# Sliding-window attention and a gated FFN on one core: half 1's steps in another order, and batch 1's last steps earlier in tile 1

## Chip, core and metric

One core of a Trainium2 chip. The metric is the device time of one execution in microseconds; the kernel before took 249.9 (median of 4 runs, 249.57 to 251.01).

## What is computed

Attention over 4 batches, 8 heads, 768 positions, 64 elements per head, where a query sees the first 8 keys and the 96 keys up to its own, with a bias by distance; then a gated feed-forward block over all 3072 tokens.

```python
scores = scale * np.matmul(q, k.transpose(0, 1, 3, 2))
bias = -slopes[:, None, None] * dist[None, :, :]
scores = np.where(keep, scores + bias[None], -1e9)      # keep = first 8 keys, or 0 <= rel < 96
a = np.exp(scores - np.max(scores, axis=-1, keepdims=True))
a = a / (np.sum(a, axis=-1, keepdims=True) + 1e-09)
attn = np.matmul(a, v)
x = attn.transpose(0, 2, 1, 3).reshape(B * S, H * D)    # 3072 x 512
g = x @ w_gate                                          # 512 x 1536
val = x @ w_val
out = (g * (1.0 / (1.0 + np.exp(-g))) * val) @ w_out    # 1536 x 512
```

## The kernel before

**Tiles.** The feed-forward block runs over 8 tiles t of 384 tokens (half a batch each: tile 2b + half) and 12 slices f of 128 hidden elements. For each (t, f) TensorE (PE) makes a gate group (`gps`, L502) and a value group (`vps`, L502), four matmuls each; ACT makes tanh of the gate (`th`, L513), DVE `sl` from it (L515) and `hT` from the value (L519). An output part is three matmuls into `ops` (L531); four parts make 128 rows, which ACT scales (`osb`, L537) and SP stores (L538). The texts write g6, v6 and o6 for the gate group, the value group and the output part of f = 6.

**Attention** works on pairs of heads (4 to a batch) and quads (2 to a batch, two pairs each). Its steps are put between the groups of the feed-forward block:

- Batch 0 comes in two halves. `trh` turns q and k of a pair in half 1 on PE (L293); DVE copies the k part (L306) and ACT the q part (L320) out of PSUM. `sch` makes the scores of a pair in half 1: bias matmuls (L329), scores (L340), four exps on ACT (L348).
- From batch 1 on `tr` (batch 1, L267) or transposing DMAs (L397) turn, `sc` makes one of three banks of scores of a pair (L365), with exps (L373) and a mask product (L381, L384).
- `va` is a quad's values for one half: denominators and two numerators on PE (L429), copies `ns` on ACT (L460), `dT` and `dR` on DVE (L439, L440), `rb` on DVE (L445), and the two products that write two of the four pieces of `xT` (L464): on DVE for batch 0, on POOL from batch 1 on. A tile's first gate group reads all four pieces of its `xT` in turn.

**What sets the order.** The program is scheduled by hand: each engine runs its instructions in the order in which the code emits them. `stretches` (L699) is a list of (groups, steps, tail, owed). In a stretch every group adds its weight (1.0, an output part 1.1) times `quota` to `owed`, and a step is emitted whenever `owed` reaches 1:

```python
        quota = len(steps) / (work - tail)
```

So a longer tail makes the steps come at shorter intervals. Parts of a step that are off PE go to the list `later`; `run_later(1)` emits one of them before each group, and all of them before a step. For `va` these are `invert` (dT, dR), then `spread` (rb, and on POOL the two products).

**Loads.** POOL issues the loads that cast to 16 bits: in the order of the code for what comes ahead of the loop (weights, batch 0, q, k and v of batch 1; L118, L152, L170, L212, L217), and by due step for batches 2 and 3. Those of batch 2 (L721 to L731) start at t = 1, f = 7: `stage_rows` (the memset of `kend` on POOL, L160; small copies of `kend` and `kst` on SP, L161 and L164) and two loads of `kst` (L193), then at each f two loads of `qst` or `kst`, and at f = 8 also one of `kend` (L198). They are emitted at the head of the gate group of that f, ahead of its `run_later`.

**PSUM.** The steps take their buffers from four banks a0 to a3 in turn (`bank`, L233), gate and value groups from three others, output parts from one.

Of the kernel before, what the change touches and what calls it, by code (L numbers as in the profile page):

```python
# [37 lines left out]
def kernel(  # L38
# [199 lines left out]
    def banks(name, dt=FP32):  # L238
        return [bank(name, dt) for _ in range(2)]
# [401 lines left out]
    def sc(b, hp, bk):  # L641
        on_vector = b < 2 or bk < 2 or hp % 2 == 0
        return lambda: pairs[b, hp].scores(bk, nc.vector if on_vector else nc.gpsimd, bool(later))

    def va(b, g, half):
        return lambda: quads[b, g].values(half, bank, nc.vector if b == 0 else nc.gpsimd)

    def tr(b, hp):
        return pairs[b, hp].transposes

    def trh(hp):
        def step():
            pairs[0, hp].transposes_half(1, [t[:, 0:TB] for t in banks("trs", FP16)], V, A)
        return step

    def sch(hp):
        def step():
            p = pairs[0, hp]
            scs = [p.bias(1, 0), p.bias(1, 1)]
            for which in range(2):  # L660
                p.scores_half(1, which, scs[which])
        return step
# [13 lines left out]
    def first(b):  # L676
        return [[tr(b, 0), tr(b, 1)], [sc(b, 0, 0), sc(b, 0, 1)], [tr(b, 2), tr(b, 3)],
                [sc(b, 1, 0), sc(b, 1, 1)], [sc(b, 2, 0), sc(b, 2, 1)], [va(b, 0, 0)],
                [sc(b, 3, 0), sc(b, 3, 1)], [], [va(b, 1, 0)]]

    def both(b):

        n = b + 1

        return [[sc(b, 0, 2), sc(b, 1, 2)], [sc(b, 2, 2), sc(b, 3, 2), fetch(n, 0, 1)],
                [va(b, 0, 1)], [va(b, 1, 1)],
                [sc(n, 0, 0), sc(n, 0, 1), fetch(n, 2, 3)], [sc(n, 1, 0), sc(n, 1, 1)],
                [va(n, 0, 0)], [sc(n, 2, 0), sc(n, 2, 1)],
                [sc(n, 3, 0), sc(n, 3, 1)], [va(n, 1, 0)]]

    half1 = [[trh(0), trh(1)], [trh(2), trh(3)], [sch(0)], [sch(1)],
             [va(0, 0, 1)], [sch(2)], [sch(3)], [va(0, 1, 1)]]

    def ff(t, f0, f1, n_out=(0,)):
        return [(t, f, n_out[(f - f0) % len(n_out)]) for f in range(f0, f1)]
# [1 line left out]
    stretches = [  # L699
        (ff(0, 0, 4), [], 0, 0),  # L700
        (ff(0, 4, 11) + [(0, 11, 3)], half1, 4.7, 0.4),
        (ff(1, 0, 12, (0, 1, 1, 1)), first(1), 5.0, 0.2),
        (ff(2, 0, 12, (1,)) + ff(3, 0, 12, (1,)), both(1), 6.0, 0.4),
        (ff(4, 0, 12, (1,)) + ff(5, 0, 12, (1,)), both(2), 6.0, 0.4),
        (ff(6, 0, 12, (1,)), second(3), 6.0, 0.4),
# [95 lines left out]
```

The softmax here doesn't subtract the row's maximum and nothing guards it: scores larger than these inputs give would overflow.

## Time and profile before

| | |
|---|---|
| time, median of 4 runs | 249.9 us |
| the profiled execution | 249.78 us |
| its span | 248.0 us |
| PE busy | 238.5 us (96%) |
| DVE, ACT, POOL busy | 159.8, 130.1, 116.3 us |
| PE clock granted | full in all slices |
| PE idle waits on transfers and xT up to 78 us, by the list of waits | q 1.4, xT 1.1, qst 0.6, vS 0.5, wg 0.2 us |

All positions are microseconds from the span's start. A timeline line gives start, duration, engine, line, operation, output and input, the count of instructions merged, and in brackets the idle time ahead of it and what ended it. A line of waits gives the total, the number of waits and the longest. A line of POOL with DMA_DIRECT2D is the issue of a transfer, not the transfer.

### The profile page before, as it was taken

What the parts mean: (1) busy time and instruction counts of PE and PEld (TensorE: products, weight loads), DVE (VectorE), ACT (ScalarE), POOL (GpSimd) and SP (SyncE); (2) the same over time, 40 slices, a digit from 0 to 9 for tenths busy, and PEclk for the clock granted to TensorE, in tenths of its full rate; (3) what the DMA queues carried; (4) which work ended last, traced back from release to release, by engine and by line L of the source; (5) the groups of instructions that cost most, each with busy time, mean ns of one, the idle gap of its engine ahead of it and who ended that gap; (6) DMA issues with size and microseconds to landing.
All of it is one profiled execution on the core that took longest, in us unless ns stands there. A gap on an engine that the chain in (4) does not pass through costs nothing.

```text
span 248.0 us, 6076 instructions
## 1 busy us (share of the span) xinstructions
PE 238.5 (96%) x2428; PEld 135.0 (54%) x2428; DVE 159.8 (64%) x346; ACT 130.1 (52%) x289; POOL 116.3 (47%) x139
## 2 busy tenths in 40 slices
PE   7997999899998999999999999999999999999994
PEld 4454555465554555555555555555555556555543
DVE  5668656678884767766775566676766666555510
ACT  5735668776753653555734734656635534332321
POOL 8898895445099924506429678603030342200000
PEclk9999999999999999999999999999999999999999
DMA  7999999999469999921919999931001101100122
GB/s 145 167 177 165 186 154 191 202 168 130 92 48 139 128 170 121 143 63 48 90 45 95 89 153 180 175 59 44 19 26 45 42 3 42 42 17 28 42 87 86
DMA packets 86644, 25.10 MB, mean 101 GB/s; under 512 B 72800, under 2 KB 83672, under 8 KB 86616
## 3 DMA queue, kind: packets, MB, share of 16 engines
q0 software_dynamic: 67472, 14.05, 69.8%
q1 hardware_dynamic: 18584, 10.30, 18.4%
q8 instruction: 19, 0.31, 0.5%
q10 hardware_dynamic: 560, 0.36, 0.5%
q14 instruction: 9, 0.07, 0.1%
HBM read 28.67 MB, written 6.29 MB: 141 GB/s over the span
## 4 chain that ended last, share of the span: by engine, by line
PE 74%; POOL 12%; DMA 11%; issue 1%; DVE 0%; ACT 0%; POOLq 0%
PE ops L531 23%; PE vps L502 21%; PE gps L502 21%; DMA qst<-in_q_dram 5%; PE sc L365 3%; DMA q<-in_q_dram 3%; DMA vS<-in_v_dram 3%; PE num L429 3%; POOL wv L212 2%; PE den L429 2%; POOL vS L170 2%; POOL wg L212 1%; POOL xT L464 1%; POOL k L118 1%; POOL qst L193 1%
## 5 line engine op out<-in xcount | busy, mean ns | idle before, releaser
L515 DVE SCALAR_TENSOR_TENSOR sl<-th,gps 128x384 f32<-128x384 f32 x94 | 52.0, 553 | 52.3 <-ACT th L513 51.5
L513 ACT ACTIVATE th<-gps 128x384 f32<-128x384 f32 x94 | 46.3, 493 | 65.9 <-PE gps L502 64.2
L502 PE MATMUL gps<-xT,wg 128*128 128x384 f16 x376 | 77.2, 326 | 1.3 <-POOL xT L464 1.1
L502 PE MATMUL vps<-xT,wv 128*128 128x384 f16 x376 | 76.6, 326 | 0.6 <-DVE sl L515 0.6
L531 PE MATMUL ops<-wo,hT 128*128 128x512 f16 x276 | 73.1, 379 | 0.0
L519 DVE TENSOR_TENSOR hT<-vps,sl 128x384 f16<-128x384 f32 x94 | 51.9, 552 | 10.1 <-PE vps L502 2.8
L464 POOL TENSOR_TENSOR xT<-ns,rb 128x384 f16<-128x384 f32 x24 | 23.9, 1015 | 69.3 <-DVE rb L445 69.3
L502 PEld LDWEIGHTS <-wg 128*128 128x128 f16 x384 | 36.3, 98 | 33.3 <-issue 1.7
L502 PEld LDWEIGHTS <-wv 128*128 128x128 f16 x384 | 36.1, 98 | 26.9 <-issue 3.2
L531 PEld LDWEIGHTS <-hT 128*128 128x128 f16 x276 | 26.2, 98 | 23.7 <-issue 0.6
L373 ACT ACTIVATE at<-sc 128x432 f16<-128x432 f32 x72 | 33.2, 535 | 9.6 <-PE sc L365 9.6
L170 POOL DMA_DIRECT2D vS<-in_v_dram x28 | 24.8, 898 | 6.5 <-DMA kst<-in_k_dram 2.4
L537 ACT ACTIVATE osb<-ops 128x512 f32<-128x512 f32 x23 | 13.7, 597 | 17.1 <-PE ops L531 17.1
L460 ACT COPY ns<-num 128x384 f32<-128x384 f32 x28 | 12.0, 482 | 9.2 <-PE num L429 8.3
L384 DVE TENSOR_TENSOR at<-at,masks 128x864 f16<-128x864 f16 x20 | 12.1, 607 | 7.0 <-ACT at L373 7.0
L193 POOL DMA_DIRECT2D kst<-in_k_dram x16 | 14.1, 888 | 0.0
L193 POOL DMA_DIRECT2D qst<-in_q_dram x16 | 13.7, 867 | 0.0
L384 POOL TENSOR_TENSOR at<-at,masks 128x864 f16<-128x864 f16 x4 | 7.3, 1820 | 13.3 <-ACT at L373 13.3
L348 ACT ACTIVATE at<-sc 128x432 f16<-128x432 f32 (+2 forms) x32 | 11.6, 446 | 3.1 <-PE sc L340 2.9
L429 PE MATMUL num<-at,vS 128*32 128x216 f16 (+6 forms) x560 | 12.3, 226 | 0.5 <-DMA vS<-in_v_dram 0.5
L439 DVE STREAM_TRANSPOSE dT<-den 128x384 f32<-128x384 f32 x16 | 9.2, 578 | 1.6 <-PE den L429 1.5
L429 PEld LDWEIGHTS <-vS 128*32 128x32 f16 x560 | 9.7, 95 | 1.0 <-DMA vS<-in_v_dram 0.7
(71 smaller groups left out, 174.8 us busy)
## 6 DMA issues: line engine op xcount, KB each, us to landing
out_dram<-osb SPq DMA_DIRECT2D x23, 256.0 KB
vS<-in_v_dram POOLq DMA_DIRECT2D x24, 120.0 KB, 6.3
wg<-in_moe_w_gate_dram POOLq DMA_DIRECT2D x12, 128.0 KB, 5.2
wv<-in_moe_w_val_dram POOLq DMA_DIRECT2D x12, 128.0 KB, 5.0
wo<-in_moe_w_out_dram POOLq DMA_DIRECT2D x4, 384.0 KB, 9.7
qst<-in_q_dram POOLq DMA_DIRECT2D x16, 96.0 KB, 4.0
kst<-in_k_dram POOLq DMA_DIRECT2D x16, 90.0 KB, 3.8
kst<-in_k_dram POOLq DMA_DIRECT2D x2, 384.0 KB, 13.4
```

What stands on the lines that cost most here:

```text
L170: nc.gpsimd.dma_start(out=vSs[b][NG:NG + n, c, :, :], in_=v[b, :, KC * c:KC * c + n, :].rearrange("h p d -> p h d"))
L193: nc.gpsimd.dma_start(out=st[b][p0:p0 + n, h // 2, :, h % 2, :], in_=src[b, h, 0:n * J].rearrange("(t p) d -> p t d", p=n))
L373: nc.scalar.activation(out=at[:, hi, :], in_=sc[hi][:, 0:BANK], func=AF.Exp, scale=scale)
L384: mul_eng.tensor_mul(at, at, m[:, :, o:o + BANK])
L429: nc.tensor.matmul(dst[r, o:o + n], lhsT=ones[:, 0:32] if side is None else vals[:, 4 * g + j, side::2], rhs=pairs[b, 2 * g + j // 2].at[c ...
L464: mul_eng.tensor_mul(self.x_out(half, side), srcs[side], self.rb)
L502: nc.tensor.matmul(gv[f, which][:, 0:TB], lhsT=w[:, c, 128 * f:128 * f + 128], rhs=x_of(t)[:, c, :], start=(c == 0), stop=(c == NC - 1))
L513: nc.scalar.activation(out=th, in_=dst[:, 0:TB], func=AF.Tanh, scale=0.5)
L515: nc.vector.scalar_tensor_tensor(out=sl, in0=th, scalar=1.0, in1=dst[:, 0:TB], op0=AluOp.add, op1=AluOp.mult)
L519: nc.vector.tensor_mul(hTs[t][:, f, :], dst[:, 0:TB], gv["sl"])
L531: nc.tensor.matmul(ops, lhsT=hTs[t][:, f, 128 * i:128 * i + 128], rhs=wo[:, f, :], start=(f == 0), stop=(f == NFF - 1))
L537: nc.scalar.mul(out=osb, in_=ops, mul=0.5)
```

## The change

Two edits in the lists that set the order.

```diff
-    half1 = [[trh(0), trh(1)], [trh(2), trh(3)], [sch(0)], [sch(1)],
-             [va(0, 0, 1)], [sch(2)], [sch(3)], [va(0, 1, 1)]]
+    half1 = [[trh(0), trh(1)], [sch(0)], [trh(2), trh(3)], [sch(1)],
+             [sch(2)], [va(0, 0, 1)], [sch(3)], [va(0, 1, 1)]]
...
     stretches = [
         (ff(0, 0, 4), [], 0, 0),
         (ff(0, 4, 11) + [(0, 11, 3)], half1, 4.7, 0.4),
-        (ff(1, 0, 12, (0, 1, 1, 1)), first(1), 5.0, 0.2),
+        (ff(1, 0, 12, (0, 1, 1, 1)), first(1), 7.0, 0.2),
```

In half 1 the slots stay where they are and the steps in them change places. In tile 1's stretch the tail goes from 5.0 to 7.0, which moves the later steps. Worked out with `quota`, the order on PE is (steps in brackets; sc2 stands for the scores of pair 2, in tile 1 its banks 0 and 1; tr for transposes, va0 for the values of quad 0):

```
half 1 before: g4 v4 [tr0 tr1] g5 [tr2 tr3] v5 g6 [sc0] v6 g7 [sc1] v7 g8 [va0] v8 g9 [sc2] v9 g10 [sc3] v10 [va1] g11 v11 o o o
half 1 after:  g4 v4 [tr0 tr1] g5 [sc0] v5 g6 [tr2 tr3] v6 g7 [sc1] v7 g8 [sc2] v8 g9 [va0] v9 g10 [sc3] v10 [va1] g11 v11 o o o
tile 1 before: ... g5 v5 o5 [sc2] g6 v6 o6 [va0] g7 v7 o7 [sc3] g8 v8 g9 [empty] v9 o9 g10 [va1] v10 o10 g11 v11 o11
tile 1 after:  ... g5 v5 [sc2] o5 g6 [va0] v6 o6 g7 [sc3] v7 o7 g8 [empty] v8 g9 v9 [va1] o9 g10 v10 o10 g11 v11 o11
```

## Prediction

> **What bounds the kernel now.** The page first: PE is busy 96% of the span, so what an edit of order can win or lose is PE's idle time. The list of PE's own waits says where that idle time is:
>
> ```profile
> PE trs L293 <- DMA q<-in_q_dram: 1.4, 3, 0.6
> ...
> PE gps L502 <- POOL xT L464: 1.1, 2, 0.6
> PE vps L502 <- DVE sl L515: 0.6, 1, 0.6
> PE trs L267 <- DMA qst<-in_q_dram: 0.6, 1, 0.6
> PE num L429 <- DMA vS<-in_v_dram: 0.5, 1, 0.5
> ...
> PE gps L502 <- DMA wg<-in_moe_w_gate_dram: 0.2, 1, 0.2
> ...
> PE den L429 <- ACT at L348: 0.2, 1, 0.2
> ```
>
> The PE timeline dates them. In half 1: 24.34 (0.65, q), 26.47 (0.39, q), 28.45 (0.20, wg), 34.86 (0.47, vS), 41.84 (0.17, exp). At the head of tile 1: 49.35 (0.63, qst). At the head of tile 2: 76.99 and 77.94 (0.44 and 0.62, xT). From 78 to 236 us the table by stage has PE busy 22.00 of 22.00 and 136.00 of 136.00. So whatever PE gains or loses up to 78 us reaches the end one to one.
>
> The two stretches end in different waits. At 49.35 the transposes of batch 1 wait for a transfer:
>
> ```profile
> 49.35 0.53 PE L267 MATMUL trs<-ident,qst 128*64 128x128 f16 x12 [0.63 <-DMA qst<-in_q_dram]
> ```
>
> At 77.94 the first gate group of tile 2 waits for the last piece of xT, which POOL makes. POOL's timeline there shows why it is late:
>
> ```profile
> 56.98 0.55 POOL L160 MEMSET kend<- 128x512 f16 x1
> 57.50 1.67 POOL L193 DMA_DIRECT2D kst<-in_k_dram  x2
> 67.87 2.32 POOL L464 TENSOR_TENSOR xT<-ns,rb 128x384 f16<-128x384 f32 x2 [8.71 <-DVE rb L445]
> 70.14 0.69 POOL L198 DMA_DIRECT2D kend<-in_k_dram  x1
> 70.82 1.68 POOL L193 DMA_DIRECT2D qst<-in_q_dram  x2
> 72.48 1.75 POOL L193 DMA_DIRECT2D kst<-in_k_dram  x2
> 74.20 1.72 POOL L193 DMA_DIRECT2D qst<-in_q_dram  x2
> 75.90 1.99 POOL L464 TENSOR_TENSOR xT<-ns,rb 128x384 f16<-128x384 f32 x2
> ```
>
> The reader is to see two things. POOL stands 8.71 us idle before the products of the first quad, since they wait for rb. From then on it has no gap: the second pair of products starts when the loads of batch 2 ahead of it have been issued (75.90), not when its rb is ready, which was at 74.73 (74.16 + 0.57 in DVE's timeline).
>
> [...] kst and qst take POOL 0.84 to 0.92 us each and land a median of 3.5 us after issue, and POOL goes on meanwhile. [...] the first pair of products took 2.32, with a mask product of DVE (L384, at 68.72) beside it; the second pair, with none, 1.99.
>
> **Part 1, half 1's order.** No instruction is added or dropped; the engines' instruction lists of the two kernels have the same lengths. The step slots stay where they are, so scores of pair 0 now run in the slot at 25.72 (g6 and v5 stand for the gate group of f = 6 and the value group of f = 5, o5 for the output part behind it), and transposes 2 and 3 in the one at 28.78. The score step is 1.10 (28.78 to 29.88), two transposes without their wait 0.99 (25.72 to 27.10, less 0.39). The scores need pair 0's and 1's copies out of PSUM: DVE's end at 25.60 and ACT's at 25.60, so no stall. Then v5 0.66 and half of g6 0.33 bring PE to 25.72 + 1.10 + 0.66 + 0.33 = 27.81; the wg half lands at 28.45, as before, since POOL issues it without waiting for PE: a wait of 0.64 in place of 0.39 + 0.20. g6 ends at 28.78 in both. From there to the end of the last values (42.73) the work was 13.95; it loses a score step (-1.10), gains two transposes (+0.99), and the vS wait goes (-0.47), as those values now come after scores of pair 2, later than 34.86. The exp wait of 0.17 I leave. Sum: 0.58 sooner, from both sides 0 to 0.8 (where PE is early it may wait for the weights of f = 10, but those had landed by its old time).
>
> On the path this is worth **nothing**. Tile 1's first step keeps its place (after three groups), and qst lands at 49.31: it is issued at 36.69 behind a fixed POOL queue and takes 12.62. PE comes at 47.62 in place of 48.20 and waits 1.21 in place of 0.63. The same 1.21 is the cover if some copy stalls half 1: up to that much is free, beyond it each us is lost.
>
> **Part 2, tail 5.0 to 7.0 in tile 1's stretch.** The groups weigh 33.9, so a step comes every (33.9 - 7)/9 = 2.99 in place of 3.21 units. Worked through, the first four steps keep their slots; scores of pair 2 move from after o5 to after v5; values of quad 0 from after o6 to after g6; scores of pair 3 from after o7 to after g7; values of quad 1 from after g10 to after v9. PE's total does not change. What moves on POOL decides: values of quad 0 pass the loads of f = 7, so the order is now products of quad 0, **then** memset and two kst loads, then the old sequence. The products of quad 1 stay behind the f = 10 loads.
>
> So the 0.55 + 1.67 = 2.19 us (56.98 to 59.17) that lay in POOL's idle time now lie behind its wait for rb: **+2.19**. Against it, rb is ready sooner. The steps, with spacings of the trace: v5 starts at 60.45; scores start 0.74 later (57.92 to 58.66): 61.19. Exps start 0.40 after (61.84 to 62.24): 61.59. In the new order all four exps stand ahead of g6's tanh, 1.64 for four (59.16 to 60.80): 63.23. sl 0.57 after (63.18 to 63.75): 63.80. The mask product 0.47 after (61.37 to 61.84, the same pair of instructions): 64.27. dT 0.59 after (64.87 to 65.46): 64.86. dT to the end of rb, in the same order as at 72.99 to 74.73, 1.74: 66.60. It was 67.72, so **-1.12**. Both ends for this: with DVE free, den ready at about 63.5 plus 1.74 gives 65.2 (-2.5); with nothing won, 0.
>
> POOL then: 66.60 + 0.15 = 66.75 start; 2.32 for the pair[...]; 2.19; 5.71 for kend and six loads (70.19 to 75.90); 1.99. End: 78.96. It was 77.89. Queued behind: PE's fourth matmul of tile 2, with all of PE after it; SP's copies of kend and kst, behind the memset, from 65.54 to about 70, ahead of the next output at 76.89, so free. PE stall in tile 2: 1.06 grows to 2.13. Nothing later absorbs it.
>
> Sum: 0 + 2.19 - 1.12 = +1.07. Against the profiled execution's 249.78 (248.0 span and 1.78 around it): **250.85**, say 250.9. The median of the four runs, 249.9, lies 0.12 above that execution, well inside their spread.
>
> **Rivals.** (A) The stall goes as the place of the step suggests: quad 1's values run 1.3 us sooner and POOL is in time; 1.06 gone, 248.7. For it: the values do move. Against it: POOL was late because of loads, not of rb, and even with DVE free the chain gives -2.5 + 2.19 = -0.3, 249.5. (B) rb is no sooner, since DVE is at 10.34 of 12.00 between 56 and 68 and the mask product goes ahead of dT: then the full 2.19 stays and the time is 252.0. It decides when rb ends at 67.7 or later. (C) The end on the faster side, through half 1: PE is 0.58 ahead and qst lands that much sooner: 250.85 - 0.58 = 250.3. Against: nothing in POOL's queue up to 56 us waits for PE.
>
> **Chances.** Forecast 0.62, own range 250.4 to 251.4; A and its weaker form 0.10; B 0.22; C 0.06. A measurement of this kernel tells about 0.5% from no change, that is 248.65 and 251.15. Of the forecast's 0.62, 0.18 lies above 251.15: slower 0.22 + 0.18 = 0.40. Of A 0.03 lies below 248.65: faster 0.03. Same 0.57. The range, 249.8 to 252.0, leaves out most of A and the tail of B.
>
> **What would show it.** Right: qst transposes still at 49.35 with a wait of about 1.2; no vS wait; POOL's order xT, memset, kst; first xT at about 66.8; xT of quad 1 ending near 79.0; two waits on xT of about 2.1 together; PE without gap afterwards. Wrong: a first xT before 65.7 (then no loss), qst transposes before or after 49.35, or a new wait after 80 us.

## The result, and the profile after

| | before | changed |
|---|---|---|
| time, median | 249.52 us (64 runs) | 250.54 us (43 runs) |
| ratio of the times | | 1.0034, 95% interval 1.0018 to 1.0050 |
| the profiled execution | 249.78 us, span 248.0 | 250.87 us, span 249.1 |
| mean granted PE clock in it | 1.000 | 0.992 |

Ratios and means of times are of executions within 1.5% of the fastest of the same kernel, unless the text says otherwise; medians and counts of low clocks take all. The change costs about 0.9 us. The sum of the prediction (+1.07, to 250.9) is near it, but not all of its terms are, as the trace shows first. PE's own waits in the changed kernel:

```profile
PE gps L502 <- POOL xT L464: 1.8, 2, 1.2
...
PE trs L293 <- DMA q<-in_q_dram: 0.9, 2, 0.7
PE vps L502 <- DVE sl L515: 0.8, 2, 0.7
PE gps L502 <- DMA wg<-in_moe_w_gate_dram: 0.7, 1, 0.7
...
PE den L429 <- ACT at L348: 0.2, 1, 0.2
```

The waits on vS and on qst are gone, the wait on wg has come as half 1's step said, and the wait on xT has grown. Why it has grown is on POOL's timeline:

```profile
54.07 1.54 POOL L170 DMA_DIRECT2D vS<-in_v_dram  x2 [1.54 <-DMA qst<-in_q_dram]
65.10 2.32 POOL L464 TENSOR_TENSOR xT<-ns,rb 128x384 f16<-128x384 f32 x2 [9.49 <-ACT th L513]
67.36 0.52 POOL L160 MEMSET kend<- 128x512 f16 x1
67.82 1.74 POOL L193 DMA_DIRECT2D kst<-in_k_dram  x2
69.55 0.65 POOL L198 DMA_DIRECT2D kend<-in_k_dram  x1
70.19 1.69 POOL L193 DMA_DIRECT2D qst<-in_q_dram  x2
71.84 1.77 POOL L193 DMA_DIRECT2D kst<-in_k_dram  x2
73.56 1.73 POOL L193 DMA_DIRECT2D qst<-in_q_dram  x2
75.25 2.01 POOL L464 TENSOR_TENSOR xT<-ns,rb 128x384 f16<-128x384 f32 x2
```

DVE's timeline has the rb of quad 0:

```profile
64.38 0.57 DVE L445 STREAM_TRANSPOSE rb<-dR 128x384 f32<-128x384 f32 x1
```

Memset and first kst loads now stand behind the products of quad 0 (67.36 to 69.55, 2.19 us), where before they lay in POOL's idle time. POOL waits 9.49 us with nothing to do, then runs without a gap to 77.26. (The releaser named, ACT's tanh, had long been done; the wait is for rb, which ends at 64.38 + 0.57 = 64.95.)

PE's timeline at the head of tile 2, in the kernel before and then in the changed one, shows the longer stall, and something that the prediction does not have:

```profile
76.07 0.49 PE L502 MATMUL gps<-xT,wg 128*128 128x384 f16 x2
76.99 0.32 PE L502 MATMUL gps<-xT,wg 128*128 128x384 f16 x1 [0.44 <-POOL xT L464]
77.94 0.32 PE L502 MATMUL gps<-xT,wg 128*128 128x384 f16 x1 [0.62 <-POOL xT L464]
78.10 0.81 PE L502 MATMUL vps<-xT,wv 128*128 128x384 f16 x4
```

```profile
74.69 0.49 PE L502 MATMUL gps<-xT,wg 128*128 128x384 f16 x2
76.36 0.32 PE L502 MATMUL gps<-xT,wg 128*128 128x384 f16 x1 [1.19 <-POOL xT L464]
77.31 0.32 PE L502 MATMUL gps<-xT,wg 128*128 128x384 f16 x1 [0.63 <-POOL xT L464]
77.47 1.29 PE L502 MATMUL vps<-xT,wv 128*128 128x384 f16 x4
78.56 1.48 PE L531 MATMUL ops<-wo,hT 128*128 128x512 f16 x3
79.84 1.43 PE L502 MATMUL gps<-xT,wg 128*128 128x384 f16 x4
81.10 0.81 PE L502 MATMUL vps<-xT,wv 128*128 128x384 f16 x4
```

The groups right behind the stall take 1.29 to 1.48 us in place of 0.81. (The bracket counts only the gap after the modelled end of the matmul before. The gate group as a whole took 78.10 - 76.07 = 2.03 us before and 77.47 - 74.69 = 2.78 in the changed kernel, against 0.65 without a wait, so a stall listed as 1.06 costs 1.38, and one of 1.82 costs 2.13.) The table by stage, with the granted clock in the column behind POOL's, says why:

```profile
core 0: us, PE busy (x) PEld busy (x) DVE busy (x) ACT busy (x) POOL busy (x), PEclk, DMA share, GB/s
77.00:77.50 0.50, 0.19 (x2) 0.12 (x2) 0.00 (x0) 0.00 (x0) 0.50 (x2) 1.00 1.51 325
77.50:81.00 3.50, 3.50 (x12) 1.50 (x11) 1.11 (x2) 0.49 (x1) 3.50 (x5) 0.52 1.22 128
81.00:81.50 0.50, 0.50 (x5) 0.27 (x3) 0.00 (x0) 0.20 (x1) 0.50 (x2) 0.92 2.22 141
```

From 77.67 to 81.08 us, 3.41 us, PE ran at half its clock (0.50 in each of the slices 78 to 79, 79 to 80 and 80 to 81). From the last xT wait to the end of the span the kernel before takes 248.0 - 77.94 = 170.06 us, the changed one 249.1 - 77.31 = 171.79: the fall costs 1.73 us. Without it this execution would have been faster than the profiled one before, and that leads to the other surprise, at the head of tile 1:

```profile
47.03 0.53 PE L267 MATMUL trs<-ident,kst 128*64 128x128 f16 x12
47.49 0.53 PE L267 MATMUL trs<-ident,qst 128*64 128x128 f16 x12
```

The transposes of q start at 47.49 without a wait. The prediction had put them at 49.35, on a landing (the moment when a transfer's data have arrived) taken for fixed.

### The profile page after: what moved, and what is told of

It is laid out like the page before. It is cut to its first block, busy times and chain, and to the rows that moved or that the text cites. A ratio compares the mean times of both kernels' runs of the same rounds, so it can differ in the third digit from the quotient of the medians.

```text
span 249.1 us, 6075 instructions
## 1 busy us (share of the span) xinstructions
PE 239.8 (96%) x2428; PEld 135.4 (54%) x2428; DVE 160.2 (64%) x346; ACT 129.8 (52%) x289; POOL 116.3 (47%) x139
## 4 chain that ended last, share of the span: by engine, by line
PE 77%; POOL 4%; issue 1%; ACT 0%
PE ops L531 24%; PE gps L502 22%; PE vps L502 22%; PE sc L365 3%; PE num L429 3%; PE den L429 2%; PE trs L267 1%; POOL qst L193 1%; POOL kst L193 1%; POOL xT L464 1%; PE ops L547 1%; POOL kend L198 0%; POOL kend L160 0%; ACT th L513 0%; ACT osb L551 0%
## 5 line engine op out<-in xcount | busy, mean ns | idle before, releaser
L502 PEld LDWEIGHTS <-wg 128*128 128x128 f16 x384 | 36.8, 98 | 35.4 <-issue 3.0
L429 PE MATMUL num<-at,vS 128*32 128x216 f16 (+6 forms) x560 | 11.9, 226 | 0.0
```

The source lines that it names most:

```text
L429: nc.tensor.matmul(dst[r, o:o + n], lhsT=ones[:, 0:32] if side is None else vals[:, 4 * g + j, side::2], rhs=pairs[b, 2 * g + j // 2].at[c ...
L502: nc.tensor.matmul(gv[f, which][:, 0:TB], lhsT=w[:, c, 128 * f:128 * f + 128], rhs=x_of(t)[:, c, :], start=(c == 0), stop=(c == NC - 1))
```

## The experiments

Three theories came out of the trace. **Loads**: the loads that POOL issues ahead of a product decide when tile 2 can start. **Clock**: a stall of PE at that place lets the clock fall in some executions. **Lead**: batch 1's q lands at varying times, so part of half 1's lead reaches the end, against the prediction's "worth nothing". In the table "low clock" counts executions with a mean granted clock of 0.993 or less: 3.41 us at half the clock take 0.7% off the mean of a span of 248 us, and the changed kernel's trace, with these 3.41 us, has 0.992. (A mean of 0.998 or 0.999 is not counted: f1's trace has 0.998, and 1.00 in the stage behind its stall, 77 to 81 us.)

| run | half 1 | tail | loads | xT stall in its trace | ratio to before, 95% interval | low clock |
|---|---|---|---|---|---|---|
| e1_same_again | old | 5 | as before | 1.1 | 1.0018 (0.9998 to 1.0037) | 5 of 22 |
| e2_half1_only | new | 5 | as before | 1.1 | 1.0001 (0.9981 to 1.0021) | 1 of 22 |
| e3_tail_only | old | 7 | as before | 1.8 | 1.0092 (1.0057 to 1.0126) | 4 of 9 |
| e4_loads_ahead | new | 7 | f = 7 at f = 6 | 0 | 0.993 (0.990 to 0.996) | 0 of 12 |
| f1_changed_again | new | 7 | as before | 1.8 | 1.0028 (1.0002 to 1.0053) | 9 of 22 |
| f2_kept_busy | new | 7 | as before | filled | 1.0015 (0.9992 to 1.0038) | 0 of 22 |
| f3_tail_loads_ahead | old | 7 | f = 7 at f = 6 | 0 | 0.9949 (0.9926 to 0.9972) | 1 of 21 |
| f4_before_loads_behind | old | 5 | f = 10 at f = 11 | 0.2 | 0.9939 (0.9917 to 0.9962) | 0 of 22 |
| g1_half1_again | new | 5 | as before | 1.1 | 0.9957 (0.9932 to 0.9982) | 0 of 22 |
| g2_ahead_again | new | 7 | f = 7 at f = 6 | 0 | 0.9898 (0.984 to 0.9955) | 0 of 6 |
| g3_ahead_old_half1 | old | 7 | f = 7 at f = 6 | 0 | 0.9952 (0.9924 to 0.998) | 0 of 17 |
| g4_behind_half1 | new | 5 | f = 10 at f = 11 | 0.2 | 0.9941 (0.9914 to 0.9968) | 0 of 19 |

The e, the f and the g runs were each made on one chip, the three on different ones.

### The two parts apart

The kernel before, unchanged (no edit):

> The kernel before, unchanged, beside itself: ratio 1.000, so its interval tells what five rounds can resolve. Its trace is a second sample of what varies from run to run. Theory 1 (the transfer of batch 1's q lands at a fixed place, 49.3 us, with PE waiting 0.6 us for it): the same wait again. Theory 2 (its landing varies by a microsecond or two between executions): another wait, or none, and everything after it shifted by that much. The clock should be full throughout, with a stall of about 1.1 us on xT at the head of tile 2.

1.0018, with an interval to 1.0037, so differences under 0.2 to 0.4% are not to be read from one such run. Its trace has the stall of 1.1 us at tile 2 and a wait for batch 1's q of 0.34 us (at 49.76), in place of 0.63.

Half 1's order alone:

```diff
-    half1 = [[trh(0), trh(1)], [trh(2), trh(3)], [sch(0)], [sch(1)],
-             [va(0, 0, 1)], [sch(2)], [sch(3)], [va(0, 1, 1)]]
+    half1 = [[trh(0), trh(1)], [sch(0)], [trh(2), trh(3)], [sch(1)],
+             [sch(2)], [va(0, 0, 1)], [sch(3)], [va(0, 1, 1)]]
```

> Half 1's new order alone, tail 5.0 as before. Theory 1 (the prediction: PE's lead of 0.6 us is lost in the wait for batch 1's q): ratio 1.000, 249.5 us. Theory 2 (that landing varies and is often earlier, so the lead counts): 0.3 to 0.6 us faster, ratio 0.998. In the trace both have g6's wait on weights at about 0.7 us, no vS wait, and the last values of half 1 about 0.6 us sooner; the stall at tile 2 stays at 1.1 us or less, and the clock stays full.

> Half 1's new order alone, again. So far 1.0001 (0.9981 to 1.0021), while six traces say that PE reaches tile 1's transposes 1 to 2 us sooner than in the old order and then waits 0.2 to 0.7 us for q. Theory 1 (the lead is lost): 1.000. Theory 2 (part of the lead counts): 0.998, and an interval below 1 when the two runs are taken together.

1.0001 and 0.9957. The second interval lies below 1, the first does not exclude theory 1; both means lie below those of the kernel before on the same chip (249.04 against 249.12, 248.68 against 249.27), the first by less than the noise. In the second run's trace one sees where the lead goes. PE's timeline:

```profile
47.33 0.53 PE L267 MATMUL trs<-ident,kst 128*64 128x128 f16 x12
48.56 0.53 PE L267 MATMUL trs<-ident,qst 128*64 128x128 f16 x12 [0.71 <-DMA qst<-in_q_dram]
...
54.35 0.53 PE L267 MATMUL trs<-ident,kst 128*64 128x128 f16 x12
55.80 0.53 PE L267 MATMUL trs<-ident,qst 128*64 128x128 f16 x12 [0.92 <-DMA qst<-in_q_dram]
```

There are two landings: that of pairs 0 and 1, and that of pairs 2 and 3 some 7 us later. PE, being early, waits at both here; in seven of the eight traces with the new order it waits at the first, in two at the second. In the profiled execution before, the second transfer had been issued at 38.94 and took 16.2 us, so it landed at 55.14, and its transposes began at 55.51: 0.37 us of slack, which the prediction did not look at.

The tail alone:

```diff
-        (ff(1, 0, 12, (0, 1, 1, 1)), first(1), 5.0, 0.2),
+        (ff(1, 0, 12, (0, 1, 1, 1)), first(1), 7.0, 0.2),
```

> Tail 7.0 alone, half 1 in the old order. Prediction's step (2.2 us of memset and loads put behind the wait for rb, rb 1.1 us sooner): the stall at tile 2 grows from 1.1 to 2.1 us, +1.1 us. With the theory formed from the changed kernel's trace (such a stall makes the TensorE clock fall to half for 3.5 us in some executions, worth 1.7 us): +1.1 without the fall and +2.8 with it, ratio 1.004 to 1.009. Rival (the stall has no part in the clock's fall, half 1's order has): +1.1 and a full clock in all runs.

1.0092, a loss of 2.3 us, with the stall of 1.8 us in its trace and a low clock in 4 of 9 executions. The loss belongs to the tail, and the rival (that half 1's order makes the clock fall) is out: half 1 is the old one here. Its size is less sure, with nine executions: the five at a full clock lie 1.7 us above those of the kernel before (250.71 against 249.05), where the trace has 1.02 us of it (from v5 to the last wait on xT 18.51 us, in place of 17.49), and two have a mean clock of 0.984 and 0.986, twice the price of the one fall that the trace of the changed kernel shows; where the rest lies was not shown.

### The loads

The changed kernel with the first loads of batch 2 a slice sooner, which puts them ahead of quad 0's products on POOL:

```diff
-        items = [(base, lambda b=b: stage_rows(b)), (base + 1, lambda b=b: load_ends(b))]
+        lead = 1 if b == 2 else 0
+        items = [(base - lead, lambda b=b: stage_rows(b)), (base + 1, lambda b=b: load_ends(b))]
...
-                    items.append((base + n / rate,
+                    items.append((base + n / rate - (lead if n < 2 else 0),
```

> The changed kernel, with the memset and the first two kst loads of batch 2 emitted at f = 6 in place of f = 7, so that on POOL they stand ahead of the products of quad 0 again, in POOL's idle time. Theory (they are what delays the last product): products of quad 1 end 2.2 us sooner, the stall at tile 2 goes from 1.8 us to 0 to 0.2, the clock stays full; about 1.8 us faster than the changed kernel where its clock held and 3.5 where it fell, so 247.7 to 248.5, ratio to before 0.993 to 0.996. Rival (the products wait for something else, rb or a copy): stall and time as in the changed kernel.

0.993: the stall and the low clocks are gone, and the kernel is faster than both. POOL's timeline in this run, then PE's:

```profile
55.43 0.55 POOL L160 MEMSET kend<- 128x512 f16 x1
55.94 1.67 POOL L193 DMA_DIRECT2D kst<-in_k_dram  x2
65.26 2.32 POOL L464 TENSOR_TENSOR xT<-ns,rb 128x384 f16<-128x384 f32 x2 [7.64 <-ACT th L513]
67.52 0.69 POOL L198 DMA_DIRECT2D kend<-in_k_dram  x1
...
73.28 2.00 POOL L464 TENSOR_TENSOR xT<-ns,rb 128x384 f16<-128x384 f32 x2
```

```profile
74.84 0.81 PE L502 MATMUL gps<-xT,wg 128*128 128x384 f16 x4
75.49 0.81 PE L502 MATMUL vps<-xT,wv 128*128 128x384 f16 x4
```

The first pair starts where it does in the changed kernel (65.26 against 65.10), the second 1.97 us sooner (73.28 against 75.25), and tile 2's first gate group goes through its four matmuls without a wait. The gate group takes 75.49 - 74.84 = 0.65 us in place of 2.78. The edit moves nothing on PE, DVE or ACT.

The kernel before has a stall of the same kind, and the same lever:

```diff
-                    items.append((base + n / rate,
+                    late = 1 if b == 2 and n in (6, 7) else 0
+                    items.append((base + n / rate + late,
```

> The kernel before, with batch 2's two qst loads of f = 10 emitted at f = 11, so that quad 1's products stand ahead of them on POOL. Neither half 1 nor the tail is changed. Theory (what makes the last piece late is POOL's queue of loads, in the kernel before too): products of quad 1 start at about 74.9, 0.15 after their rb, in place of 75.9; PE waits for the third piece no more and for the fourth 0 to 0.3 us in place of 1.1 in all; about 0.9 us faster, ratio 0.996. Rival (the values' place on PE is what decides): the stall stays at 1.1 us, ratio 1.000.

0.9939, with 0.17 us left of the stall. POOL's timeline:

```profile
71.70 1.75 POOL L193 DMA_DIRECT2D kst<-in_k_dram  x2
74.09 1.97 POOL L464 TENSOR_TENSOR xT<-ns,rb 128x384 f16<-128x384 f32 x2 [0.64 <-DVE rb L445]
76.01 1.74 POOL L193 DMA_DIRECT2D qst<-in_q_dram  x2
```

Here the second pair is the one that waits for rb, and POOL is idle ahead of it. So in the kernel before, too, it was loads and not the place of the values on PE that made the last piece late. The gate group took 0.99 us (75.29 to 76.28) in place of 2.03, so 1.04 us went; the gain of 1.5 us (0.95 to 2.1 by the interval) is not clearly more. Low clocks can add little: 6 of 74 executions of the kernel before on this chip had one, at 1.1 us each, which is 0.1 us in the mean.

### The clock

The changed kernel again, and the same with PE kept busy where it waits. The useless matmuls compute nothing of the output:

```diff
+                if (t, f, which) == (2, 0, 0):
+                    products(2, 0, 0, 0, 2)
+                    keep_busy(10)
+                    products(2, 0, 0, 2, 3)
+                    keep_busy(5)
+                    products(2, 0, 0, 3, 4)
+                    gate_or_val(t, f, which, NC)
...
+        for _ in range(n):
+            nc.tensor.matmul(idle["ps"][:, 0:256], lhsT=ones[:, 0:128], rhs=ones[:, 0:256],
+                             start=True, stop=True)
```

> The changed kernel, unchanged, for a second interval and a second trace: 1.0034 to before, as on record. Theory (its stall at tile 2 makes the clock fall in some executions): about 4 executions in 10 with a mean granted clock of 0.993 or less, these some 1.2 us slower than the others. In the trace a stall of about 1.8 us on xT, wherever batch 1's q lands.

> The changed kernel, with matmuls without use (10 and 5 of 128x256, about 1.1 and 0.55 us) on a free PSUM bank between the second, third and fourth matmul of tile 2's first gate group, where PE waits for the last two pieces of xT. They compute nothing of the output. Theory (idle PE lets the clock fall): the pieces still come 1.8 us late, but no execution has a mean clock of 0.993 from here, and the mean time falls by the clock's share, 0.4 x 1.7 = 0.7 us, to a ratio of about 1.001. Rival (the clock falls for another reason, so PE's idle time is innocent): the share of slow-clock executions stays at 4 in 10 and the time at 1.003; the useless matmuls may then add up to 0.2 us.

The changed kernel measured 1.0028 this time, with 9 of 22 executions at a low clock: these took 251.96 us in the mean of all, the 13 others 249.97. Its profiled execution is one of the others. PE's timeline there:

```profile
76.24 0.32 PE L502 MATMUL gps<-xT,wg 128*128 128x384 f16 x1 [1.19 <-POOL xT L464]
77.19 0.32 PE L502 MATMUL gps<-xT,wg 128*128 128x384 f16 x1 [0.63 <-POOL xT L464]
77.35 0.81 PE L502 MATMUL vps<-xT,wv 128*128 128x384 f16 x4
78.00 0.81 PE L531 MATMUL ops<-wo,hT 128*128 128x512 f16 x3
```

The stall is the same to 0.01 us, yet the groups behind it take 0.81. From the last wait to the end it is 247.3 - 77.19 = 170.1 us, as in the kernel before. So the same stall lets the clock fall at one time and not at another.

With the useless matmuls no execution of 22 had a low clock, though the pieces of xT came as late as ever:

```profile
74.41 0.49 PE L502 MATMUL gps<-xT,wg 128*128 128x384 f16 x2
74.73 1.26 PE L715 MATMUL idle<-ones 128*128 128x256 f16 x10
76.09 0.32 PE L502 MATMUL gps<-xT,wg 128*128 128x384 f16 x1
76.25 0.71 PE L715 MATMUL idle<-ones 128*128 128x256 f16 x5
77.04 0.32 PE L502 MATMUL gps<-xT,wg 128*128 128x384 f16 x1
```

The rival (idle PE is innocent) had said 9 of 22 as before. In these runs the clock therefore falls because of PE's idle time (9 of 22 executions with it, 0 of 22 with it filled), not because of late data. What the falls cost is less sure. The theory had said 0.7 us; the mean fell from 250.79 to 250.06 over all executions, from 250.36 to 249.96 over those within 1.5%, and the two intervals of the ratio overlap. Over all runs with a listed clock, the kernels with a stall of 1.8 us have 30 low clocks in 75 executions, those with 1.1 us (the kernel before among them) 19 in 243, those with 0 to 0.2 us 1 in 97. No kept trace of the last two kinds holds a fall, so where theirs lies is not shown.

What decides whether the clock falls is not shown. The traces around tile 2's first gate group:

| trace | PE idle there | behind it |
|---|---|---|
| changed kernel | 1.82 us | clock 0.50 from 77.67 to 81.08 us; groups of 1.29 to 1.48 us |
| e3_tail_only | 1.82 us | groups of 1.21 to 1.49 us from 80.34 on |
| f1_changed_again | 1.82 us | clock 1.00 from 77 to 81 us; groups of 0.81 us |
| before | 1.06 us | clock 1.00 from 78 to 100 us; groups of 0.81 us |
| e1_same_again | 1.06 us | groups of 0.81 us |
| e2_half1_only | 1.05 us | groups of 0.81 us |

### What half 1's order is worth

> The version with the loads ahead of quad 0's products, but half 1 in the old order: it tells what half 1's order is worth where the stall at tile 2 is gone. Theory 1 (the lead is lost in the wait for batch 1's q): the same as with the new order, ratio 0.993. Theory 2 (the lead counts): up to 0.6 us slower than with the new order, ratio 0.9955. The stall at tile 2 is 0 to 0.2 us in both, and the clock full.

> The changed kernel with batch 2's first loads ahead of quad 0's products, again, on one chip with its counterpart below: 0.993, stall at tile 2 of 0 to 0.2 us, full clock in all executions.

> The same with half 1 in the old order, 0.9949 before. Against the run above it gives half 1's worth where nothing at tile 2 waits. Theory 1: no difference. Theory 2: 0.002 slower than the run above.

> The kernel before with the two qst loads of f = 10 behind quad 1's products (0.9939) and half 1 in the new order; the tail is 5.0. Theory 1: 0.994. Theory 2: 0.992, the fastest of all, since half 1's lead is no longer lost on any later wait. If it equals the run with tail 7.0 and the loads ahead, the tail has no worth of its own.

With the loads ahead the new order gave 0.993 and 0.9898, the old one 0.9949 and 0.9952. Each pair of intervals overlaps, and the 0.9898 is from 6 executions (by their mean, 247.60 us against 249.27 of the kernel before, it would be 0.993); the new order is ahead both times, and once more in the changed kernel against the tail alone (1.0034 and 1.0028 against 1.0092, whose intervals do not overlap). With the loads behind, the two orders cannot be told apart (0.9941 and 0.9939). Theory 2 (part of the lead counts) has more for it than theory 1, but its size isn't settled: where nothing at tile 2 stalls, the points lie between about nothing (loads behind) and 0.8 us (247.60 against 248.38, loads ahead on one chip). The forecast of a fastest version at 0.992 was missed: tail 5.0 with the loads behind comes out like tail 7.0 with the loads ahead, so the tail has no worth of its own that these runs show.

The traces show what becomes of the lead. In the new order PE comes to tile 1's transposes between 45.81 and 47.75 us (8 traces), in the old one between 48.20 and 49.34 (6 traces); the old one pays a wait for vS of 0.4 to 1.3 us in all six of its traces, the profiled one before having one of the smallest. The transposes of the first q then start between 46.51 and 48.94 in the new order, nearly always after a wait of 0.2 to 0.7 us, and between 48.69 and 50.48 in the old, in four of six after a wait too. So in 11 of 14 traces their start is set by the landing of q, whatever the lead; that the landing itself comes sooner because of the new order is not shown.

## Why the prediction was right or wrong

- **Part 2, POOL's order: right in each term.** From v5's start to the end of rb the forecast had 66.60 - 60.45 = 6.15 us; it is 64.95 - 58.80 = 6.15. The first pair took 2.32, memset and kst loads 2.19, the sequence up to the second pair 5.70 (69.55 to 75.25) against 5.71, the second pair 2.01 against 1.99. Only the starting point lay 1.65 us sooner. So the first xT came at 65.10, which the prediction had named as a sign of no loss ("before 65.7"), and the loss came all the same: that sign took PE's own arrival as fixed, and PE was early by as much. The run with the loads ahead shows POOL's order from the other side.
- **"PE stall in tile 2: 1.06 grows to 2.13": a term mis-sized, its sum right.** It grew to 1.82, by 0.76. PE itself came later by 0.27 us (v5 to the gate group of tile 2: 15.89 in place of 15.62), most of it a group that waited at 68.47 for a buffer that DVE had not read yet; DVE's mask products just ahead (66.95) had taken 1.00 us, in place of 0.67 at 70.38 in the kernel before; POOL's first pair ran to 67.42 and its memset to 67.88, and whether that is the cause was not tried. From v5 to the last wait on xT it is 18.51 us (58.80 to 77.31) in place of 17.49 (60.45 to 77.94): +1.02, where the forecast had +1.07.
- **"So whatever PE gains or loses up to 78 us reaches the end one to one": the step that failed.** A stall cost more than its length where the clock fell behind it: 1.73 us more in the profiled execution; 17 of 44 executions of the changed kernel had a low clock. Neither the sum nor a rival had it, and the profile of before, with a full clock in all slices, gave no sign of it.
- **"On the path this is worth nothing": the second step that failed.** It rested on one landing, 49.31, read as fixed because POOL's queue does not wait for PE. But the landing moves from one execution to the next: the transfer took between 10.5 and 14.0 us over 14 traces. In the profiled pair v5 came 1.65 us sooner, where the forecast had nothing. How much of that half 1's order gives in the mean stays open; the runs without a stall at tile 2 have it between nothing and 0.8 us. The waits named (0.64 on wg for 0.39 and 0.20, vS gone, exp 0.17 left) came as worked out: 0.69, none, 0.17.
- **"Sum: 0.58 sooner": half 1's lead, mis-sized.** PE came to tile 1's transposes at 47.03 in place of 48.20, 1.17 us sooner. The forecast took each wait at its listed idle time, and two waits cost more than that. The numerators of quad 0, listed with 0.47 us of wait, took 1.53 us (34.01 to 35.54); without it 0.71 (36.13 to 36.84), so 0.82 went. The two transposes, put at 1.38 - 0.39 = 0.99, took 0.79 (28.80 to 29.59), so the wait listed with 0.39 had cost 0.59.
- **The sum was right because two misses cancel: luck.** In the profiled pair PE is at v5 1.65 us sooner (forecast 0), takes 1.02 longer from there to the last wait on xT (forecast 1.07), and loses 1.73 behind it to the clock (forecast 0): -1.65 + 1.02 + 1.73 = +1.10, the difference of the spans. Over many executions both misses are smaller, as the landing moves and the clock falls only at times. On the chip of the f runs the changed kernel is 0.75 us above the kernel before (250.36 against 249.61), and 0.35 with PE kept busy (249.96), so about half of its loss there goes with the low clocks, within a noise of some 0.6 us.
- **Rivals.** A (the stall goes) was wrong for the reason given, loads and not rb. B (rb no sooner) was wrong. C (qst lands sooner, so that half 1's gain reaches the end) came true in the profiled execution; over the runs it holds in part at most.

## What to carry to other kernels

POOL both computes and issues transfers here, and its timeline is one queue: when a step that waits was moved ahead of transfers that used to lie in its wait, their issue time (2.19 us with the memset) moved onto the path, and moving these transfers took it off again at no cost that the runs show. So look at what an engine does during a wait before moving the step that waits. A transfer's landing read from one trace is a sample (10.5 to 14.0 us after issue in 14 traces here); a gain should be judged lost or kept only against its spread. And a stall of PE is to be priced with what the clock may do behind it: the same 1.82 us brought 1.73 us more in one trace of the changed kernel and nothing in the other.

## What was not expected of the hardware

- The clock fell to half for 3.41 us (77.67 to 81.08) behind 1.82 us of PE idle time in the changed kernel's trace, and stayed full behind the same 1.82 us in f1's; what decides was not shown. In the kernels with that stall 30 of 75 executions had a low clock. The price was 1.73 us in the trace; between the means of all executions with and without a low clock it was 2.0 us in f1 and 1.2 in the 44 executions of the changed kernel.
- The same POOL transfer of q took 10.5 to 14.0 us over 14 traces of kernels that issue it in the same order, issued between 35.4 and 37.1 us. With half 1 in the new order it took 10.5 to 11.9, in the old 10.8 to 14.0. Whether that difference is chance or has a cause on the chip was not tried.
